# The four feature buffers of a token-mixing kernel start 32 bytes higher in each partition

## The chip, the cores and the metric

The kernel runs on one core of a Trainium2 chip. The metric is the device time of one execution in microseconds (us). Two executions of the kernel before took 2963.32 and 2964.55 us; the median is 2963.94 us.

## The reference

Three layers follow one another on x of 4 batches, 4224 tokens and 192 channels, all in float32:

```python
out = np.einsum('hk,bskhg->bshg', w, x_unf)          # 7 taps along the tokens, softmaxed
theta = x @ w_theta
zr, zi = x * np.cos(theta), x * np.sin(theta)
y = np.einsum('ts,bsd->btd', w_tok_r, zr) + np.einsum('ts,bsd->btd', w_tok_i, zi)
u = x + y; x = u + np.maximum(u @ w_ch, 0.0)
h = x.transpose(0, 2, 1) @ U @ V                     # rank 32 along the tokens
u = x + h.transpose(0, 2, 1)
out = u + np.maximum(u @ w_ch1, 0.0) @ w_ch2
```

The bulk is the token mix: two 4224 x 4224 matrices times 768 columns (4 batches of 192 channels). The weights come as float64, and the kernel turns them into float32 itself.

## The kernel before

Every large product is made of three products of halves of the numbers: a value is split into a high part (rounded to the matmul's input format, fp32r) and a low part (what is left), and high times high, high times low and low times high are added up.

**The token mix.** The 4224 source tokens are 33 blocks of 128. A unit of preparation (lines 421 to 590) takes one block and one half of the batches: the taps (L452), the product with w_theta (L515 to L519), the sine and cosine, and the rotated features z with their high and low parts (L574, L577). The features of a block go to one of four feature buffers, a pool named zp (L272), each 128 partitions by 3072 words of 4 bytes. The matrices w_tok come in by DMA, are turned from float64 into float32 by ScalarE and VectorE in four passes (L224 to L243), and are split into w (L626, L629), two buffers of 3840 words.

A step takes two blocks of source tokens and one range of 464 or 480 target tokens (WIDTHS, L34). For each of six slots of 128 columns, `products` (L671) makes twelve matmuls into one PSUM tile: z is the stationary operand, 128 x 128, loaded by an LDWEIGHTS of its own before each matmul, and w is the moving operand, 464 or 480 columns long. The twelve are four triples, in this order: z high with w high, the same z high with w low, z low with w high.

```python
for a, b in ((zh, high), (zh, low), (zl, high)):                     # L682
    mm(ps, a, b[:, i + r, :], start=n == 0, stop=n == last)          # L683
```

VectorE then adds the PSUM tile to the running sum yt (L691). The last steps of the mix are 384 wide (LATE); their weights are laid out otherwise (weight_part, L595 to L605), and between their matmuls stands the work of the layer's end: the product with w_ch (L842 to L844 and L872 to L876), the transposes (L892) and the projection by U (L912).

**The final stage** has 22 units of 384 tokens: 12 products up with w_ch1 (`up_mm`, L1165 to L1169: w stationary, the features fq moving) and 12 down with w_ch2 (`down`, L1200 to L1204: cl stationary, hid moving), five matmuls each, all 384 columns wide.

**Where the tiles lie in a partition.** Tiles are placed by pools. The pools cst, yp, wp and wraw grow from the low end, and the pools on the right side grow down from the high end: first a spacer named room (L271) that nothing reads or writes, then zp with its four buffers, then the preparation's tiles (prep), in whose place the tiles of the end of the mix (post) are put later. The tile hid lies on the left side, behind a spacer of its own (L1258).

In the following, a place is a word's number counted modulo 64 words of 4 bytes (256 bytes). In the built program the two w buffers start at byte 118496 and 133856 of a partition, both word 56 of 64. With rows of 480 words in the order of weight_part (L598), the low parts of w start at word 56 and the high parts at word 24. In the 384-wide steps, w starts at word 0 (L603); the weights of the products up start at word 8 (L605); hid starts at word 40. The four feature buffers start at bytes 180064, 192352, 204640 and 216928, all word 24, and so do all slices of 128 and 384 words in them.

Nothing sets the order of the work but the order in which it is written: the table OPENING for the first steps, the loop `mix` (L761) with a plan by slot for the middle, the tables ENTRY and TURN for the end.

Of the kernel before, what the change touches and what calls it, by code (L numbers as in the profile page):

```python
# [10 lines left out]
F32 = mybir.dt.float32  # L11
# [7 lines left out]
P = 128  # L19
# [179 lines left out]
def mix_kernel(ctx, tc, xT, wcv, wth, wtok, wch, uu, vv, w1, w2, outT):  # L199
# [3 lines left out]
    def pool(name, bufs=1, side=None, space=None, stack=None):  # L203
        kw = dict(name=name, bufs=bufs, reuse_waits="tile")
        if side:
            kw["side"] = side
        if space is not None:
            kw["space"] = space
        return (stack or ctx).enter_context(tc.tile_pool(**kw))
# [51 lines left out]
    right = ExitStack()  # L261
# [6 lines left out]
    wp = pool("wp", bufs=2, stack=left)  # L268
    wrp = pool("wraw", bufs=2, stack=raw_st)

    pool("room", side="right", stack=right).tile([P, 32], F32, name="room")  # L271
    zp = pool("zp", bufs=4, side="right", stack=right)  # L272
    pp = pool("prep", side="right", stack=prep_st)
    ps_mm = pool("ps_mm", bufs=4, space=PSUM)
# [1141 lines left out]
```

## Time and profile before

| what | value |
|---|---|
| median of two executions | 2963.94 us |
| the profiled execution | 2963.67 us |
| its span, first to last instruction | 2961.9 us |
| TensorE busy in the span | 2948.1 us, 14994 matmuls |
| weight loads busy | 2693.9 us, 14994 |
| VectorE busy | 2495.3 us |
| ScalarE busy | 1554.3 us |
| GpSimd busy | 291.8 us |
| mean granted TensorE clock | 1.000 |

PE is TensorE's matmuls and PEld its weight loads, which run beside the matmuls; DVE is VectorE, ACT is ScalarE, POOL is GpSimd. Matmuls are pipelined: the record of one goes on after the next has started, so the time that a matmul really takes from the stream is the distance from its start to the start of the next.

### The profile page before, as it was taken

Reading aid. Unit: us, or ns where it says so; the run is one execution under the profiler, and the core shown is the slowest. Engines: PE = TensorE matmul, PEld = TensorE weight load, DVE = VectorE, ACT = ScalarE, POOL = GpSimd, SP = SyncE. Lnnn points to the kernel's source line nnn. Section 1 sums busy time; section 2 is a strip of 40 time slices with the busy share of each in tenths; the row PEclk is TensorE's granted clock in tenths of the full one; section 3 lists DMA queues with packets and bytes.
Section 4 is the critical chain, followed back from the end, with each engine's and each line's share of the span. In section 5 each row is a group of like instructions: output and inputs, shape, how many; then the busy total and the mean of one; then the engine's idle time right before and its main releaser. Section 6 shows DMA issues by size and latency. Waiting matters only on the chain.

```text
span 2961.9 us, 39012 instructions
## 1 busy us (share of the span) xinstructions
PE 2948.1 (100%) x14994; PEld 2693.9 (91%) x14994; DVE 2495.3 (84%) x4133; ACT 1554.3 (52%) x2237; POOL 291.8 (10%) x254
## 2 busy tenths in 40 slices
PE   9999999999999999999999999999999999999999
PEld 8888888888888989898989898988889999999999
DVE  8799989888888888898989898989899897555555
ACT  7655545455555555554555554545456555444443
POOL 2110000010000000000000010100002002000000
PEclk9999999999999999999999999999999999999999
DMA  4443443443434434434334344343433221101110
GB/s 137 132 132 123 127 133 124 127 132 122 137 123 128 133 124 130 130 123 135 124 125 135 123 128 131 124 135 127 125 127 116 65 62 52 38 31 43 35 38 33
DMA packets 119002, 323.50 MB, mean 109 GB/s; under 512 B 6688, under 2 KB 40480, under 8 KB 118688
## 3 DMA queue, kind: packets, MB, share of 16 engines
q1 hardware_dynamic: 118416, 320.81, 33.6%
q8 instruction: 118, 1.93, 0.3%
q14 instruction: 68, 0.56, 0.1%
q10 hardware_dynamic: 400, 0.21, 0.0%
HBM read 308.01 MB, written 12.98 MB: 108 GB/s over the span
## 4 chain that ended last, share of the span: by engine, by line
PE 95%; DVE 4%; ACT 1%; issue 0%; DMA 0%; POOL 0%; DVEq 0%; POOLq 0%
PE acc L683 73%; PE ob L1201 2%; PE acc L1165 2%; PE acc L1169 2%; PE acc L1166 2%; PE oa L1202 2%; PE ob L1200 2%; PE oa L1204 2%; PE oa L1203 2%; PE acc L1167 2%; PE acc L1168 2%; PE pacc L912 1%; PE th L515 1%; PE th L516 1%; DVE yt L691 1%; PE th L518 1%
## 5 line engine op out<-in xcount | busy, mean ns | idle before, releaser
L683 PE MATMUL acc<-w,z 128*128 128x464 f32 (+2 forms) x10836 | 2287.3, 371 | 2.6 <-DVE yt L691 0.8
L683 PEld LDWEIGHTS acc<-w,z 128*128 128x128 f32 x10836 | 2018.7, 188 | 240.6 <-DVE yt L691 1.7
L691 DVE TENSOR_TENSOR yt<-acc,yt 128x464 f32<-128x464 f32 (+2 forms) x876 | 550.3, 634 | 213.3 <-PE acc L683 210.7
L626 ACT CAST w<-wraw 128x928 fp32r<-128x928 f32 (+3 forms) x291 | 303.5, 1043 | 635.1 <-DVE wraw L243 634.9
L238 DVE TENSOR_SCALAR wraw<-wraw 128x928 uint16<-128x928 uint16 (+4 forms) x305 | 368.8, 1210 | 11.8 <-ACT wraw L229 6.3
L629 DVE TENSOR_TENSOR w<-wraw,w 128x928 fp32r<-128x928 f32 (+2 forms) x282 | 365.0, 1294 | 0.0
L224 ACT ACTIVATE wraw<-wraw,consts 128x928 int32<-128x928 uint16 (+4 forms) x305 | 348.8, 1144 | 20.5 <-DMA wraw<-in_wtok 15.8
L243 DVE SCALAR_TENSOR_TENSOR wraw<-wraw 128x928 int32<-128x928 int32 (+4 forms) x305 | 342.0, 1121 | 10.1
L229 ACT ACTIVATE wraw<-wraw 128x928 f32<-128x928 f32 (+3 forms) x296 | 310.2, 1048 | 3.7 <-DMA wraw<-in_wtok 2.9
L577 POOL TENSOR_TENSOR z<-tz,z 128x384 fp32r<-128x384 f32 x121 | 125.2, 1034 | 1706.3 <-ACT z L574 1706.3
L452 DVE SCALAR_TENSOR_TENSOR xa<-xr,tap,xa 128x256 f32<-128x256 f32 x744 | 285.6, 425 | 0.0
L1177 DVE SCALAR_TENSOR_TENSOR hid<-acc,hid 128x384 fp32r<-128x384 f32 x264 | 146.9, 557 | 149.3 <-ACT hid L1174 148.3
L1174 ACT ACTIVATE hid<-acc 128x384 fp32r<-128x384 f32 x264 | 129.8, 492 | 250.2 <-PE acc L1169 233.8
L574 ACT CAST z<-tz 128x384 fp32r<-128x384 f32 x129 | 66.2, 513 | 289.4 <-DVE tz L563 289.3
L583 POOL TENSOR_TENSOR yt<-yt,xa 128x384 f32<-128x384 f32 x64 | 70.2, 1097 | 248.6 <-DVE xa L452 195.4
L1201 PE MATMUL ob<-hid,cl 128*128 128x384 f32 x264 | 89.2, 338 | 0.1
L1165 PE MATMUL acc<-fq,w 128*128 128x384 f32 x264 | 89.2, 338 | 0.0
L1169 PE MATMUL acc<-fq,w 128*128 128x384 f32 x264 | 89.0, 337 | 0.0
L1202 PE MATMUL oa<-hid,cl 128*128 128x384 f32 x264 | 88.8, 336 | 0.0
L1204 PE MATMUL oa<-hid,cl 128*128 128x384 f32 x264 | 88.8, 336 | 0.0
L1203 PE MATMUL oa<-hid,cl 128*128 128x384 f32 x264 | 88.8, 336 | 0.0
L1200 PE MATMUL ob<-hid,cl 128*128 128x384 f32 x264 | 88.7, 336 | 0.0
(239 smaller groups left out, 2655.2 us busy)
## 6 DMA issues: line engine op xcount, KB each, us to landing
wraw<-in_wtok SPq DMA_DIRECT2D x184, 928.0 KB, 4.7
wraw<-in_wtok SPq DMA_DIRECT2D x92, 960.0 KB, 4.9
wraw<-in_wtok SPq DMA_DIRECT2D x22, 768.0 KB, 4.4
xr<-in_xT SPq DMA_DIRECT2D x63, 201.0 KB, 2.6
outT<-ot SPq DMA_DIRECT2D x20, 576.0 KB, 3.0
vzw<-in_vv SPq DMA_DIRECT2D x10, 384.0 KB, 4.1
wraw<-in_w SPq DMA_DIRECT2D x3, 768.0 KB, 4.3
yt<-in_wtok SPq DMA_DIRECT2D x2, 928.0 KB, 8.8
```

What stands on the lines that cost most here:

```text
L224: nc.scalar.activation(words(raw, 0), words(raw, 1, U16), AF.Identity, scale=2.0**-13, bias=consts[:, 3:4])
L229: nc.scalar.activation(w, w, AF.Copy, scale=2.0**-112)
L238: nc.vector.tensor_scalar(out=words(raw, 1, U16), in0=words(raw, 3, U16), scalar1=0x8000, scalar2=None, op0=ALU.bitwise_and)
L243: nc.vector.scalar_tensor_tensor(out=words(raw, 1), in0=words(raw, 1), scalar=3, in1=words(raw, 0), op0=ALU.logical_shift_left, op1=ALU.bi ...
L452: nc.vector.scalar_tensor_tensor(out=xa, in0=src, scalar=w, in1=xa, op0=ALU.mult, op1=ALU.add)
L626: nc.scalar.copy(hi, src)
L629: eng.tensor_tensor(out=weight_part(g, q, 1), in0=src, in1=f(hi), op=ALU.subtract)
L683: mm(ps, a, b[:, i + r, :], start=n == 0, stop=n == last)
L691: nc.vector.tensor_tensor(out=dst, in0=ps, in1=dst, op=ALU.add)
L1165: mm(ps, w[0], q[:, b, :], start=True, stop=False)
L1169: mm(ps, w[3], q[:, 4 + b, :], start=False, stop=True)
L1201: mm(ob, c2[:, m, 2, :], h[:, 1, :], start=False, stop=last)
```

## The change

One number: the spacer on the right side is 24 words instead of 32.

```diff
-    pool("room", side="right", stack=right).tile([P, 32], F32, name="room")
+    pool("room", side="right", stack=right).tile([P, 24], F32, name="room")
     zp = pool("zp", bufs=4, side="right", stack=right)
     pp = pool("prep", side="right", stack=prep_st)
```

In the built program all tiles of zp, prep and post start 32 bytes (8 words) higher. The feature buffers start at bytes 180096, 192384, 204672 and 216960, word 32 of 64. All else stays where it was: w, wraw, yt, hid, the constants and the tiles in PSUM. No instruction is added, removed or moved on any engine or queue.

## Rows read from the trace of the kernel before

**Rows 1.** The page, part 1: busy time, share of the span, instructions.

```profile
span 2961.9 us, 39012 instructions
PE 2948.1 (100%) x14994; PEld 2693.9 (91%) x14994; DVE 2495.3 (84%) x4133; ACT 1554.3 (52%) x2237; POOL 291.8 (10%) x254
```

**Rows 2.** The waits of PE: line, whom it waited for: us, times, longest.

```profile
PE pacc L912 <- DVE u2s L902: 1.7, 5, 0.8
...
PE acc L683 <- DVE yt L691: 0.8, 1, 0.8
PE acc L683 <- POOL z L577: 0.7, 1, 0.7
```

**Rows 3.** Windows: stretch, its us, busy us and instructions by engine, granted clock, DMA.

```profile
1000.00:1100.00 100.00, 100.00 (x486) 89.12 (x485) 90.13 (x145) 52.91 (x67) 8.10 (x8) 1.00 0.40 131
...
2700.00:2800.00 100.00, 100.00 (x579) 100.00 (x578) 57.56 (x108) 44.06 (x88) 7.40 (x4) 1.00 0.13 42
```

**Rows 4.** Groups, shapes apart: count | busy us, mean ns of one | idle before.

```profile
L683 PE MATMUL acc<-w,z 128*128 128x464 f32 x6696 | 1411.5, 371 | 0.9 <-DVE yt L691 0.8
L683 PE MATMUL acc<-w,z 128*128 128x480 f32 x3348 | 731.7, 379 | 1.0 <-POOL z L577 0.7 <-ACT z L574 0.2
L683 PE MATMUL acc<-w,z 128*128 128x384 f32 x792 | 149.8, 340 | 0.7 <-DVE yt L880 0.7
L1165 PE MATMUL acc<-fq,w 128*128 128x384 f32 x264 | 89.2, 338 | 0.0
L1201 PE MATMUL ob<-hid,cl 128*128 128x384 f32 x264 | 89.2, 338 | 0.1
```

**Rows 5.** Timeline of PE, merged, mix: start us, us, line, shapes, count.

```profile
1145.82 30.28 PE L683 MATMUL acc<-w,z 128*128 128x464 f32 x144
...
1208.62 46.90 PE L683 MATMUL acc<-w,z 128*128 128x480 f32 x216
```

**Rows 6.** Groups of PE, one 464-wide triple, three windows with one record each.

```profile
L683 PE MATMUL acc<-w,z 128*128 128x464 f32 x1 | 0.4, 371 | 0.0
...
L683 PE MATMUL acc<-w,z 128*128 128x464 f32 x1 | 0.4, 367 | 0.0
...
L683 PE MATMUL acc<-w,z 128*128 128x464 f32 x1 | 0.4, 376 | 0.0
```

**Rows 7.** The same, two 480-wide triples: the distinct durations.

```profile
L683 PE MATMUL acc<-w,z 128*128 128x480 f32 x1 | 0.4, 382 | 0.0
...
L683 PE MATMUL acc<-w,z 128*128 128x480 f32 x1 | 0.4, 373 | 0.0
...
L683 PE MATMUL acc<-w,z 128*128 128x480 f32 x1 | 0.4, 379 | 0.0
...
L683 PE MATMUL acc<-w,z 128*128 128x480 f32 x1 | 0.4, 375 | 0.0
```

**Rows 8.** Timeline of PE, merged, a 384-wide step with the layer's end.

```profile
2349.37 2.25 PE L683 MATMUL acc<-w,z 128*128 128x384 f32 x12
...
2353.03 0.33 PE L872 MATMUL acc<-uz,cz 128*128 128x384 f32 x1
...
2353.90 2.28 PE L683 MATMUL acc<-w,z 128*128 128x384 f32 x12
```

**Rows 9.** DMA issues into a moved tile: count, KB each, median us to landing.

```profile
xr<-in_xT SPq DMA_DIRECT2D x63, 201.0 KB, 2.6
```

## The prediction

> **What bounds the kernel now.** I began with the busy times: PE is busy in 2948.1 of 2961.9 us [rows 1]. Next I read whom PE waited for: its longest sum is 1.7 us, and the mix line L683 shows waits of under 1 us each [rows 2]. Then the windows: the granted clock is 1.00 in the mix and in the final stage, PE is busy in all of each 100 us, and the next engine, VectorE, stands at 90.13 us in the mix and 57.56 us in the final stage [rows 3]. So the time is the sum of the distances between matmul starts, and nothing else ends last. With no instruction moved, the change can act only by making these distances longer or shorter.
>
> **What a matmul costs above its columns.** [...] An unbroken run of 144 matmuls of 464 takes 30.28 us [rows 5]; its last one lies 371 ns long in the record [rows 4], so one takes (30.28 - 0.37) / 143 = 209.2 ns: 15.9 ns above its columns. A run of 216 of 480 gives (46.90 - 0.38) / 215 = 216.4 ns, 16.4 ns above [rows 4, 5]. In both, a record is 162 ns longer than the distance to the next start (371 - 209.2, 379 - 216.4), so a single record's length, less 162 ns and less its columns, is the excess of that one matmul.
>
> Single records show that the excess depends on the operands. While one matmul streams w, the weight load of the next reads z, so each record has a pair of places: w's start and z's start. In the 464-wide triple, w high beside z high (both at word 24) lasts 371 ns, an excess of 15.7; w low (word 56) beside z low (24) lasts 367, excess 11.7; w high (24) beside the next z high (24) lasts 376, excess 20.7 [rows 6]. The mean, 16.0, agrees with the run's 15.9. In two 480-wide triples the six records last 382, 373, 379 and 382, 382, 375 ns [rows 7]: excesses of 20, 11, 17 and 20, 20, 13, mean 16.8 beside the run's 16.4. Equal starts therefore cost 18.2 ns on average at 464 and 17.5 at 480; starts half of 64 words apart cost 11.7 at 464 and 15.5 (11 and 20) at 480.
>
> Two more distances are in the rows. In the 384-wide steps w starts at word 0 and z at 24, 40 of 64 apart: (2.25 - 0.34) / 11 = 173.6 ns, 13.6 above the 160.0 of 384 columns [rows 4, 8]. In the final stage fq (24) streams beside w (8), and hid (40) beside cl (24), both 16 apart: 100 us hold 579 matmuls, 172.7 ns each, 12.7 above [rows 3].
>
> **What the change does, part by part.** It removes, adds and reorders nothing; it shifts the places of z, fq, cl, cz and the preparation's tiles by 8 words.
>
> First, the wide mix, 6696 + 3348 matmuls of L683. The pairs 24/24 become 24/32, 56 (or minus 8) of 64 apart; the pairs 56/24 become 56/32, 24 apart. No row shows either distance. For 24 I take 13.6 ns, since 16 and 40 on both sides cost 12.7 and 13.6. For 8 words from equal I take half way between equal and 13.6: 15.9 at 464, 15.6 at 480; this is a choice, an estimate from the rows named. A 464 triple then goes from 48.1 (15.7 + 11.7 + 20.7) to 15.9 + 15.9 + 13.6 = 45.4 ns, 2.7 less; 2232 triples give 6.0 us. A 480 triple goes from 50.5 (half of 101 for the six) to 15.6 + 15.6 + 13.6 = 44.8, 5.7 less; 1116 triples give 6.4 us.
>
> Second, the 792 matmuls of the 384-wide steps go from 40 to 32 apart. The rows for 32 are 11.7 and 15.5, mean 13.6: no change. The 1320 products up go from 16 to 24 apart, again 13 or so on either side: no change. The 1320 products down go from 16 to 8 apart. Equal starts at 384 columns are to be seen where uz and cz are read (both at 24): the five from L872 to L876 take 2353.90 - 2353.03 = 0.87 us, 174 ns each, 14.0 above [rows 8]. Half way from 12.7 to 14.0 is 0.65 ns more, times 1320 is 0.9 us lost.
>
> Third, what isn't on the path. VectorE's and ScalarE's work on moved tiles hides below PE: of each 100 us VectorE has 9.9 idle in the mix [rows 3]. If its work on them grew beyond that, PE would begin to wait in L683 for the additions of L691. The 63 loads of xr land 2.6 us after issue [rows 9] and are issued five slots ahead, each slot 12 matmuls of over 200 ns, so over 12 us: hidden. I cost all of this at nothing.
>
> The sum is -6.0 - 6.4 + 0.9 = -11.5 us. The profiled execution took 2963.67 us, 0.27 below the median 2963.94, so both give 2952 us.
>
> **Bounds.** From below: the whole wide mix at the cheapest 464 record, 11.7 ns, is 6696 x 4.2 + 3348 x 4.7 = 44 us less, 2920 us. From above: all of it at the dearest frequent 480 record, 20 ns, is 6696 x 4.1 + 3348 x 3.6 = 40 us more, 3003 us.
>
> **The rivals.** (a) *The starts don't matter.* Then the differences between records come from something else that repeats with the triple, such as the order high, low, high, and the time stays 2964 us. For it: w high beside z at equal places costs 15.7 once and 20.7 once, and a w low row costs 11 in one 480 triple and 20 in the other although its place modulo 64 is the same [rows 6, 7]; the pair of places alone doesn't explain the records. Equal starts at 384 cost only 14.0 [rows 8]. Against it: the lower 464 record is the one whose starts differ. [...]
>
> (b) *The new pairs are the dear ones.* [...] It decides from a mean excess above 16.1 ns in the wide mix on. For it: all six 480 records range between 11 and 20 with so little that differs between them, and nothing in the rows covers 24 or 56 apart. Against it: the rows at 16 and 40 apart lie at 12.7 and 13.6.
>
> (c) *Beyond every row.* Slower by over 2%, 59 us, needs 5.9 ns more on each of the 10044 wide matmuls, a mean of 22 ns; only single records come near. Faster by over 2% needs a mean of about 10.2 ns, below the cheapest record of 11.
>
> **How the numbers follow.** I give the forecast, a small gain between some 5 and 44 us, 0.40; rival (a), within 5 us, 0.25; rival (b), slower by 5 to 59 us, 0.22; (c) beyond 2% slower 0.09, beyond 2% faster 0.04. The point is that of the forecast, 2952 us. The range takes the two bounds, 2920 to 3003 us, which leaves a little under 2 in 10 outside, since the likely excesses lie within the rows. The likeliest case has a range of its own, 2920 to 2959 us. A measurement can tell about 2% from no change; within that lie the forecast, (a) and (b), 0.87 together.
>
> **What would show it.** In the changed profile the run of 144 matmuls of 464 should take about 30.16 us (0.9 ns less each) and the run of 216 of 480 about 46.5 us (1.9 less). By (a) they stay 30.28 and 46.90; by (b) they go to about 30.87 and 47.7. The records of a triple should draw together: w high to about 371 and w low to 369 ns at 464. The final stage should keep about 579 matmuls in 100 us. PE should still wait for nobody; a sum of waits of over 5 us in L683 would mean that VectorE's work on moved tiles grew, and that the argument looked at the wrong engine. The forecast is wrong if the runs lengthen, or if they shorten to below 29.7 us (464), which needs less than 11.7 ns a matmul.

## The result and the profile after

The changed kernel takes 2998.25 us (median of 2997.71 and 2998.79), the kernel before 2963.94 us: a ratio of 1.0114, 95% interval 1.0098 to 1.0131. It is slower by 34 us, less than 2%. The forecast of a small gain was wrong in sign.

The page of the changed kernel, part 1 (columns as in [rows 1]):

```profile
span 2997.0 us, 39012 instructions
PE 2983.2 (100%) x14994; PEld 2700.6 (90%) x14994; DVE 2497.7 (83%) x4133; ACT 1553.8 (52%) x2237; POOL 291.3 (10%) x254
```

PE is busy 35.1 us longer with the same 14994 matmuls; the weight loads beside them are busy 6.7 us longer, VectorE, ScalarE and GpSimd as long as before, within 2.4 us. No wait of PE grew by more than 0.4 us (the first of these rows stood at 1.6 us before):

```profile
PE tr L892 <- DVE u2s L902: 2.0, 4, 1.0
...
PE acc L683 <- POOL z L577: 0.8, 1, 0.8
...
PE acc L683 <- DVE yt L691: 0.5, 1, 0.5
```

The groups of matmuls of the changed kernel (count | busy us, mean ns of one | idle before), which answer [rows 4], say where the 35 us are:

```profile
L683 PE MATMUL acc<-w,z 128*128 128x464 f32 x6696 | 1432.9, 374 | 0.5 <-DVE yt L691 0.5
L683 PE MATMUL acc<-w,z 128*128 128x480 f32 x3348 | 738.0, 381 | 1.1 <-POOL z L577 0.8 <-ACT z L574 0.3
L683 PE MATMUL acc<-w,z 128*128 128x384 f32 x792 | 150.4, 340 | 0.7 <-DVE yt L880 0.7
```

Beside [rows 4], the 464-wide matmuls of the mix take 21.4 us more (1432.9 - 1411.5), the 480-wide 6.3 us (738.0 - 731.7), the 384-wide 0.6 us. The rest is the final stage: 100 us hold 570 matmuls where they held 579 [rows 3]:

```profile
1000.00:1100.00 100.00, 100.00 (x482) 88.28 (x481) 88.70 (x142) 53.67 (x70) 10.14 (x10) 1.00 0.39 123
2700.00:2800.00 100.00, 100.00 (x570) 100.00 (x569) 59.15 (x111) 46.88 (x92) 9.28 (x5) 1.00 0.10 32
```

That is 175.4 instead of 172.7 ns each, 2.7 ns on some 2640 products, 7.1 us, an estimate from one stretch. The sum is 35.4 us; PE's busy time rose by 35.1. The granted clock is 1.00 in both stretches.

The runs of the mix without a break, as in [rows 5]:

```profile
1158.64 30.74 PE L683 MATMUL acc<-w,z 128*128 128x464 f32 x144
...
1222.36 47.31 PE L683 MATMUL acc<-w,z 128*128 128x480 f32 x216
```

What the columns alone take, the matmuls alone of the experiments show: from its first start to the next run's, a cheapest run of 24 took 4.16 us at 384 columns (1352.85 to 1357.01 in the grid below), 4.96 at 464 and 5.12 at 480 (123.81 to 128.77 and 169.89 to 175.01 under the shorter loads), so 173.3, 206.7 and 213.3 ns a matmul. That is 40.0 ns for 96 columns, 0.417 ns a column, and the 464 lie on the same line. Columns of 160.0, 193.3 and 200.0 ns are worked out from this, an estimate that takes the cheapest excess, 13.3 ns, to be equal at the three widths.

With these, (30.74 - 0.37) / 143 = 212.4 ns, an excess of 19.0 above the columns where it was 15.9; (47.31 - 0.38) / 215 = 218.3, an excess of 18.3 where it was 16.4. This is rival (b), nearly at its price for 464 (30.87 us for the run of 144).

The three records of one 464-wide triple of the changed kernel, taken as those of [rows 6] were:

```profile
L683 PE MATMUL acc<-w,z 128*128 128x464 f32 x1 | 0.4, 371 | 0.0
...
L683 PE MATMUL acc<-w,z 128*128 128x464 f32 x1 | 0.4, 374 | 0.0
...
L683 PE MATMUL acc<-w,z 128*128 128x464 f32 x1 | 0.4, 375 | 0.0
```

They drew together, as the prediction had it, but at the dear end: the cheap record of w low, 367 ns before, is gone.

### The profile page after: what moved, and what is told of

It reads as the page before. It is cut to its first block, busy times and chain, and to the rows that moved or that the text cites. A ratio compares the mean times of both kernels' runs of the same rounds, so it can differ in the third digit from the quotient of the medians.

```text
span 2997.0 us, 39012 instructions
## 1 busy us (share of the span) xinstructions
PE 2983.2 (100%) x14994; PEld 2700.6 (90%) x14994; DVE 2497.7 (83%) x4133; ACT 1553.8 (52%) x2237; POOL 291.3 (10%) x254
## 4 chain that ended last, share of the span: by engine, by line
PE 95%; DVE 3%; DMA 1%; ACT 1%; issue 0%; SPq 0%; POOL 0%; DVEq 0%; ACTq 0%
PE acc L683 73%; PE acc L1166 2%; PE ob L1200 2%; PE acc L1165 2%; PE ob L1201 2%; PE acc L1167 2%; PE acc L1168 2%; PE oa L1204 2%; PE oa L1203 2%; PE acc L1169 2%; PE oa L1202 2%; PE pacc L912 1%; PE th L515 1%; PE th L516 1%; PE th L518 1%; PE tr L892 1%
## 5 line engine op out<-in xcount | busy, mean ns | idle before, releaser
L683 PE MATMUL acc<-w,z 128*128 128x464 f32 (+2 forms) x10836 | 2315.7, 374 | 2.3 <-POOL z L577 0.8
L691 DVE TENSOR_TENSOR yt<-acc,yt 128x464 f32<-128x464 f32 (+2 forms) x876 | 551.1, 635 | 237.9 <-PE acc L683 235.2
L224 ACT ACTIVATE wraw<-wraw,consts 128x928 int32<-128x928 uint16 (+4 forms) x305 | 349.0, 1144 | 22.0 <-DMA wraw<-in_wtok 17.7
L1166 PE MATMUL acc<-fq,w 128*128 128x384 f32 x264 | 89.8, 340 | 0.0
L1165 PE MATMUL acc<-fq,w 128*128 128x384 f32 x264 | 89.5, 339 | 0.0
L1204 PE MATMUL oa<-hid,cl 128*128 128x384 f32 x264 | 89.2, 338 | 0.0
L1167 PE MATMUL acc<-fq,w 128*128 128x384 f32 x264 | 89.1, 338 | 0.0
L1168 PE MATMUL acc<-fq,w 128*128 128x384 f32 x264 | 89.1, 337 | 0.0
```

What stands on the lines that cost most here:

```text
L224: nc.scalar.activation(words(raw, 0), words(raw, 1, U16), AF.Identity, scale=2.0**-13, bias=consts[:, 3:4])
L691: nc.vector.tensor_tensor(out=dst, in0=ps, in1=dst, op=ALU.add)
L1165: mm(ps, w[0], q[:, b, :], start=True, stop=False)
L1166: mm(ps, w[0], q[:, 2 + b, :], start=False, stop=False)
```

## The experiments

Three theories stood at the start. D: the two read streams of TensorE, the weight load's and the moving operand's, interfere, and the distance of their starts decides how much. Z: the place of z alone decides. O: other engines' reads and writes slow TensorE.

### Matmuls alone, at every pair of places

The kernel has two resident tiles and nothing but weight loads and matmuls from them:

```python
    for n in (464, 480, 384):
        for zp in PLACES:                      # 0, 8, ... 56
            for wp in range(0, 128, 8):
                ...                            # 24 pairs of starts: z at zp, w at wp
                a = run(f"n{n}z{zp}w{wp}e", pairs, n)
...                                            # and for 464 and 480, z at 0 to 120:
                pairs += [(zh, hi), (zh, lo), (zl, hi)]     # 24 times, so 72 matmuls
```

> A kernel that does nothing of the reference but matmuls: one weight load and one matmul after another from two resident tiles, no other engine at work meanwhile. Runs of 24 at every pair of places (z at 0 to 56 of 64, w at 0 to 120 of 128) for 464, 480 and 384 columns, and the triples of the mix (w high at 24, low at 56) for every place of z. Theory D (the two read streams of TensorE meet each other, and the distance of their starts decides): the excess above the columns is the same along lines of equal distance, differs between them by several ns, and the triples give about 15.9 ns at z 24 and 19.2 at z 32 with 464 columns. Theory Z (the place of z alone decides): the excess differs by rows of z and not by w. Theory O (TensorE is slowed by what other engines and DMAs read and write): every run has the same excess, some 3 to 12 ns, whatever the places.

The timeline of PE, merged (start us, us, line, tile, shapes, count); the tile's name says the columns and the places, so n464z24w56e is 464 columns, z at 24, w at 56 (a constant run), and t464z24e is the triple of the mix with z at 24:

```profile
286.30 5.18 PE L46 MATMUL n464z24w24e<-w,z 128*128 128x464 f32 x24
...
306.53 5.22 PE L46 MATMUL n464z24w56e<-w,z 128*128 128x464 f32 x24
...
367.31 5.13 PE L46 MATMUL n464z32w24e<-w,z 128*128 128x464 f32 x24
...
387.41 5.27 PE L46 MATMUL n464z32w56e<-w,z 128*128 128x464 f32 x24
...
1352.85 4.33 PE L46 MATMUL n384z0w16e<-w,z 128*128 128x384 f32 x24
1357.01 4.40 PE L46 MATMUL n384z0w24e<-w,z 128*128 128x384 f32 x24
...
1365.47 4.40 PE L46 MATMUL n384z0w40e<-w,z 128*128 128x384 f32 x24
...
1912.55 15.36 PE L46 MATMUL t464z16e<-w,z 128*128 128x464 f32 x72
1927.74 15.20 PE L46 MATMUL t464z24e<-w,z 128*128 128x464 f32 x72
1942.78 15.44 PE L46 MATMUL t464z32e<-w,z 128*128 128x464 f32 x72
...
2064.21 15.44 PE L46 MATMUL t464z96e<-w,z 128*128 128x464 f32 x72
...
2156.14 15.99 PE L46 MATMUL t480z16e<-w,z 128*128 128x480 f32 x72
2171.97 15.76 PE L46 MATMUL t480z24e<-w,z 128*128 128x480 f32 x72
2187.57 15.89 PE L46 MATMUL t480z32e<-w,z 128*128 128x480 f32 x72
```

With the record's length taken off as before, the triple costs an excess of (15.20 - 0.37) / 71 - 193.3 = 15.5 ns with z at 24 and 18.9 with z at 32 for 464 columns, and 16.6 and 18.5 for 480. The kernels' runs gave 15.9 and 19.0, 16.4 and 18.3. No other engine worked meanwhile:

```profile
200.00:300.00 100.00, 100.00 (x477) 89.04 (x476) 0.00 (x0) 0.00 (x0) 0.00 (x0) 1.00 0.00 0
```

So O falls. The loss in the mix is TensorE's own, and the grid gives it to within 0.4 ns a matmul. The place counts modulo 64: the triple with z at 96 takes the same 15.44 us as with z at 32. Over the whole grid of constant runs the means, from start to start after the first eight, repeat along lines of equal distance; for 464 columns, z at 0 and w at 64, 72, ... 120, they are 15.6, 17.7, 16.5, 19.9, 17.7, 19.1, 20.0 and 13.3 ns above the columns, and each further row of z has the same numbers shifted by one place. (The first runs of a row are off by up to 1.2 ns; why isn't shown.)

What the grid took away from the prediction is its price list. In constant runs w high beside z before, 24/24, costs (5.18 - 0.37) / 23 - 193.3 = 15.8 ns, and w low beside z, 56/24, costs 17.5: the reverse of the single records, where the equal start was dear and the half distance cheap. At 480 columns the order is that of the records: 16.4 and 13.3 after the first eight. The new 24/32 is among the cheapest at 464, 13.6, and 56/32 among the dearest, 19.7. If pairs had prices, the new triple would cost (13.6 + 13.6 + 19.7) / 3 = 15.6; it costs 18.9.

For 384 columns the same reckoning gives (4.33 - 0.34) / 23 - 160.0 = 13.5 ns at 16 words apart, but 16.5 at 24 and at 40. The products up go from 16 to 24 apart, so the grid has them dearer.

### Both streams up by 8 words

```diff
+    pool("lead", stack=left).tile([P, 8], F32, name="lead")
     wp = pool("wp", bufs=2, stack=left)
```

on top of the change: w, wraw and hid move with z, fq and cl.

> The changed kernel with a spacer of 8 words ahead of w too, so that w, wraw and hid also start 8 words higher: all distances between z and w, fq and w, hid and cl are those of before, only the places differ. Theory D: 2964 us, runs of 144 matmuls of 464 at 30.28 us. Theory Z: 2998 us, 30.74 us. Theory O: between them or 2998.

2962.67 us, beside 2964.47 for the kernel before on the same chip; the runs of the mix as before. (One execution of each; thirteen of the kernel before, taken later on another chip, lie between 2962.12 and 2965.67 us.)

```profile
1113.64 30.28 PE L684 MATMUL acc<-w,z 128*128 128x464 f32 x144
...
1207.80 46.90 PE L684 MATMUL acc<-w,z 128*128 128x480 f32 x216
```

z lies at word 32 as in the changed kernel, and the whole loss is gone. Z falls: word 32 is no worse than word 24; what was lost was the distance to the other stream. The two rows are, to the hundredth, those of [rows 5].

### Only w up, and z further up

The same spacer on the kernel before, so that z stays at 24:

```diff
+    pool("lead", stack=left).tile([P, 8], F32, name="lead")
     wp = pool("wp", bufs=2, stack=left)
```

> The kernel before (z at word 24) with w, wraw and hid 8 words higher: w high at 32, low at 0, hid at 48. Distances of w from z are 8 and 40 where before has 0 and 32 and the changed kernel 56 and 24. Theory D: neither 2964 nor 2998 by need, but what the triple of distances 8 and 40 gives in the grid. Theory Z: 2964 us, since z stays at 24. Theory O: 2964.

2992.71 us: z has not moved, and 28 us are lost. The distances of this triple are those of the grid's triple with z at 16, whose excess is 17.8 ns at 464 and 20.0 at 480 (here and below from start to start after the first eight). From 15.6 and 16.6 at z 24 this gives 6696 x 2.2 = 14.7 and 3348 x 3.4 = 11.4 us. The groups of this kernel rose by 14.1 (1425.6 - 1411.5) and 11.1 us (742.8 - 731.7); the rest is about what the final stage lost, which holds 573 matmuls in 100 us:

```profile
L684 PE MATMUL acc<-w,z 128*128 128x464 f32 x6696 | 1425.6, 373 | 0.2 <-DVE yt L692 0.2
L684 PE MATMUL acc<-w,z 128*128 128x480 f32 x3348 | 742.8, 382 | 1.1 <-POOL z L578 0.8 <-ACT z L575 0.3
```

And the spacer of 16 words, which puts z at 40:

```diff
-    pool("room", side="right", stack=right).tile([P, 24], F32, name="room")
+    pool("room", side="right", stack=right).tile([P, 16], F32, name="room")
```

> The changed kernel with a spacer of 16 words: z at word 40 of 64, w as before, distances 48 and 16. If the excess grows with how far z is moved up from 24, this is slower than 2998 us; if z at 32 is a single bad place, near 2964; the grid's triple at z 40 tells which, by theory D.

2969.23 us, with runs of 30.27 and 46.91 us: the mix costs what it did at 24, as the grid's 15.6 and 16.7 for z at 40 say, and of the 5 us more some 3 are the final stage's (575 matmuls in 100 us, 1.2 ns more on 2640) and 1.1 the 384-wide steps' (150.9 us busy, before 149.8). So there is no slope upwards from 24; z at 32 lies between two good places.

### The final stage held at its distances

```diff
-            return t[:, 2 * WSTEP * q + 16 : 2 * WSTEP * q + 16 + 2 * COLS]
+            return t[:, 2 * WSTEP * q + 24 : 2 * WSTEP * q + 24 + 2 * COLS]
...
-            fo.tile([P, 112], F32, name="room", tag="room")
+            fo.tile([P, 120], F32, name="room", tag="room")
```

on top of the change: the weights of the products up, and hid, move by 8 words too.

> The changed kernel (z at 32), with the weights of the products up 8 words higher and hid 8 words higher: in the final stage the distances of before, 16, come back; the mix stays as changed. Theory D: what the final stage lost, 570 instead of 579 matmuls in 100 us over its 2640 products up and down, some 6 to 7 us, is won back: 2991 us; the wide runs stay at 30.74 and 47.31 us. Theory Z: 2998 us.

2991.07 us, 7.2 less than the changed kernel. In the final stage 579 matmuls fit in 100 us again, and the run of 144 stays at 30.74 us:

```profile
2700.00:2800.00 100.00, 100.00 (x579) 100.00 (x578) 60.54 (x114) 46.34 (x92) 9.28 (x5) 1.00 0.10 34
```

The loss of 34 us is thus split by a run: 7 us in the final stage, 27 in the mix.

### Two places forecast from the grid

Without the spacer z starts at word 56, with one of 56 words at word 0; in both kernels the weights of the products up and hid are moved so that the final stage keeps its distance of 16. For z at 56:

```diff
-    pool("room", side="right", stack=right).tile([P, 24], F32, name="room")
...
-            return t[:, 2 * WSTEP * q + 16 : 2 * WSTEP * q + 16 + 2 * COLS]
+            return t[:, 2 * WSTEP * q + 48 : 2 * WSTEP * q + 48 + 2 * COLS]
...
-            fo.tile([P, 112], F32, name="room", tag="room")
+            fo.tile([P, 144], F32, name="room", tag="room")
```

For z at 0 the spacer is 56 words, the offset in the second edit 56 and the third 88.

> No spacer: z at word 56, with the final stage held at its distances of 16. The grid's triples give 15.5 ns at both widths for z 56, where z 24 gave 15.6 and 16.6. Theory D: 6696 x -0.1 and 3348 x -1.1 ns from 2964 us: 2960 us, runs of 144 and 216 of 30.27 and 46.7 us. Theory Z: not to be said.

> A spacer of 56 words: z at word 0, the final stage again held at 16. The grid's triples give 20.0 ns at 464 and 18.9 at 480, the dearest place for 464. Theory D: 6696 x 4.4 + 3348 x 2.3 ns = 37 us above 2964: 3001 us, runs of 30.9 and 47.4 us.

They took 2959.61 and 2998.63 us, 0.4 and 2.4 us off what the grid had foretold. z at 56, then z at 0:

```profile
1144.00 30.27 PE L682 MATMUL acc<-w,z 128*128 128x464 f32 x144
...
1206.79 46.68 PE L682 MATMUL acc<-w,z 128*128 128x480 f32 x216
```

```profile
1130.78 30.91 PE L683 MATMUL acc<-w,z 128*128 128x464 f32 x144
...
1226.78 47.37 PE L683 MATMUL acc<-w,z 128*128 128x480 f32 x216
```

The kernel with z at 56 was timed again in three rounds:

> z at word 56 with the final stage at its distances of 16, timed against the kernel before. Theory D: the 4 to 5 us of the first look stay, a ratio of 0.9984. If the first look was chance: 1.000.

2959.29 us beside 2963.70, a ratio of 0.9985, interval 0.9975 to 0.9994. It beats both kernels, by 0.15% and 1.3%; of its gain of 4.4 us on the kernel before, 3.0 us are in the 480-wide steps (728.7 us busy instead of 731.7), as forecast.

### Shorter loads, and other layouts

> Matmuls alone again, nothing of the reference. First, constant runs with weight loads of 128, 64 and 32 columns at eight distances, 464 and 480 columns moving. Theory D (the load's read stream and the moving stream meet): with 64 columns to load the spread over the distances, 13.3 to 20 ns with 128, shrinks to about half, with 32 to about a quarter, and the lowest value falls too. Theory Z' (only the start addresses cost, some fixed time at the beginning of a load): the spread stays near 7 ns whatever the load's length. Second, triples in which the low part lies at 0 to 56 words from the high part and every other block's row at 0 or 32: if distances alone decide, some layout comes near the lowest constant run, 13.3 ns, in both widths, where the kernel's layout gives 15.6 and 16.6.

The edit: constant runs whose stationary operand has 64 or 32 columns (m64, m32 in the names), and triples with other distances of the low part.

```profile
58.38 5.27 PE L46 MATMUL n464m128w48e<-w,z 128*128 128x464 f32 x24
63.49 5.13 PE L46 MATMUL n464m128w56e<-w,z 128*128 128x464 f32 x24
...
93.64 5.13 PE L46 MATMUL n464m64w40e<-w,z 128*64 128x464 f32 x24
...
108.65 5.28 PE L46 MATMUL n464m32w0e<-w,z 128*32 128x464 f32 x24
...
123.81 5.12 PE L46 MATMUL n464m32w24e<-w,z 128*32 128x464 f32 x24
128.77 5.21 PE L46 MATMUL n464m32w32e<-w,z 128*32 128x464 f32 x24
...
169.89 5.28 PE L46 MATMUL n480m128w32e<-w,z 128*128 128x480 f32 x24
175.01 5.39 PE L46 MATMUL n480m128w40e<-w,z 128*128 128x480 f32 x24
...
2017.49 10.93 PE L46 MATMUL t480r0h40d24e<-w,z 128*128 128x480 f32 x48
```

A miss for D as I had pictured it. With 32 columns to load, the dearest and the cheapest of eight runs of 24 still lie 0.16 us apart (5.28 and 5.12), with 128 columns 0.14 (5.27 and 5.13); the lowest excess stays at 13.3 ns. So the cost isn't a number of meetings in proportion to what the load reads. Z' had the spread right. But at 464 the cheapest distance moves with the load's length (56 words with 128 columns, 40 with 64, 24 among others with 32), so the starts alone don't set the cost either. No run leaves the load out, so how much of the 13.3 ns is its doing isn't shown. Of the 128 triples tried in each width, the best for the kernel's mixture of widths (15.4 ns at both) would save 1 us over z at 56; no layout came near 13.3 at both widths, a second miss. The dearest triple lies above every constant run: (10.93 - 0.39) / 47 - 200.0 = 24.3 ns, with w high at 40 and w low 24 words further.

### The order of the triple

> Matmuls alone, nothing of the reference: the triple in three orders (high-high, high-low, low-high as in the kernel; high-high, low-high, high-low; high-low, high-high, low-high), w low 32 words from w high, z low at 0 to 56 words from z high, eight places of w. If each pair of places had a price of its own, the order would change nothing: the mean of a triple would be the same in all three orders. If a matmul's delay depends on what went before it, the orders differ by some ns at the same places. A layout with a mean near 13.3 ns in both widths would be worth 10044 x 2.3 ns = 23 us to the kernel; the layouts so far stop at 15.5.

```profile
219.86 10.35 PE L46 MATMUL o464p0h16z24e<-w,z 128*128 128x464 f32 x48
...
1019.79 10.19 PE L46 MATMUL o464p1h32z16e<-w,z 128*128 128x464 f32 x48
...
1514.73 10.09 PE L46 MATMUL o464p2h16z24e<-w,z 128*128 128x464 f32 x48
...
1666.62 10.39 PE L46 MATMUL o464p2h32z16e<-w,z 128*128 128x464 f32 x48
...
2482.70 10.41 PE L46 MATMUL o480p0h48z8e<-w,z 128*128 128x480 f32 x48
...
3819.88 10.61 PE L46 MATMUL o480p2h48z8e<-w,z 128*128 128x480 f32 x48
```

The name gives the columns, the order (p0 as in the kernel, p1 with its last two swapped, p2 high-low first), w high's distance from z high, and z low's. The same three matmuls at the same places cost (10.35 - 10.09) / 47 = 5.5 ns a matmul less in another order, and at 480 columns (10.61 - 10.41) / 47 = 4.3 ns more.

This alone doesn't refute a price for w's start with that of the z loaded beside it, which is the pair that the prediction meant: with z low elsewhere than z high, another order also loads another z beside each w. The grid's triples refute it, where all of z lies at one place (15.6 by prices, 18.9 measured). So does a comparison inside this run. Repeated, p1 and p2 are one and the same cycle, begun at another member. In most layouts they cost the same; but with w high at 32 and z low at 16 they lie (10.39 - 10.19) / 47 = 4.3 ns a matmul apart, with the same places in the same sequence. A pair of places has no price of its own: what a matmul costs depends on what came before it, and even on how the run began.

Some layouts reach 13.4 ns at one width, none at both; the best, w high at 16 and z low at 24 in order p2, gives 13.4 at 464 and 17.0 at 480, some 9 us below z at 56 over the wide mix, by these prices. It wasn't tried in the kernel, where z low would need 24 words more in each feature buffer and a stride of the buffers that keeps their places.

## Why the prediction was wrong

**What bounds the kernel** was right. PE's waits stayed within 0.4 us, the clock stayed at 1.00, and the time moved by what the distances between matmul starts moved.

**The cost above the columns** was read rightly as a mean: 15.9 and 16.4 ns, which matmuls alone reproduce as 15.5 and 16.6. No row ahead of the prediction shows what it took off for the columns; the matmuls alone showed it afterwards, 0.417 ns a column, which gives the same 193.3, 200.0 and 160.0 ns.

**The price of a pair** is the step that failed: "Equal starts therefore cost 18.2 ns on average at 464 and 17.5 at 480; starts half of 64 words apart cost 11.7 at 464 and 15.5 (11 and 20) at 480." Within a triple, one record's delay and the next one's belong together, and only the sum over a repeating triple is a cost. At 464 constant runs of the same pairs have the reverse order (15.8 and 17.5), their prices put the new triple at 15.6 where it costs 18.9, and the same cycle of places costs 4.3 ns more or less by how it began. The warning was in the rows and was named under rival (a): the same pair 24/24 at 15.7 and 20.7 in one triple. It was used against the size of the effect and not against the price list.

**The interpolation** built on it: 15.9 for a start 8 words off and 13.6 for 24 words. Over the places of 8 words the excess isn't smooth at all: in constant runs of 464 columns neighbouring distances jump from 13.3 to 20.0 ns. There was nothing to interpolate; 24 apart, taken as the cheapest, is one of the dearest (19.9 at 464, 20.0 at 480). The forecast of -6.0 and -6.4 us became +21.4 and +6.3.

One of its two supports was also misread. The 13.6 for 40 words apart came from a single 384-wide step of 2.25 us; the other step in [rows 8], of 2.28 us, gives (2.28 - 0.34) / 11 - 160.0 = 16.4, and the grid's constant run at 40 apart 16.5.

**The 384-wide steps**, forecast at no change, took 0.6 us more. **The products up and down**: forecast at 0 and 0.9 us lost, together they lost 7. It is the same interpolation: "13 or so on either side" for the products up, 24 apart, where the grid has 16.5. What the products down lost, 8 apart, the constant runs don't show (13.3 ns at 8 as at 16); that part stays open.

**What isn't on the path** stayed off it, as forecast: VectorE's busy time rose by 2.4 us, and the waits for the additions of L691 went from 0.8 to 0.5 us.

**The rivals.** (a) fell, since both_up_8 and the grid show that the starts matter: in the grid z's place alone moves a constant run of 464 columns between 13.3 and 20.0 ns with no other engine at work. (b) held, in its direction and nearly in its price: the mix at 19.0 and 18.3 ns against the 20 that its runs of 30.87 and 47.7 us suppose. That 2998 us came so near 3003, the time with the whole wide mix at 20 ns, is in part luck, since that prices the mix alone, which lost 28 of those 40 us (21.4 + 6.3), and the final stage added 7. Why the new pairs are dear is not shown: the distance of the two starts moves the excess between 13.3 and 20.0 ns, but loads of 32 columns leave the spread of a run at 0.16 us where 128 have 0.14. What makes the excess is left open. (c) did not come up; the range of 2920 to 3003 held the time, though its upper bound, 20 ns for every wide matmul, was no limit (24.3 ns in one triple above).

## What to carry to other kernels

In this kernel, which the matmuls bound (PE busy in 2948.1 of 2961.9 us) and where loads and matmuls follow one another without a gap, the place of each operand within 64 words was a tuning knob of about 1% (2959.29 us with z at 56, 2998.63 with z at 0), and it acted by the distance of the stationary from the moving operand: z's side moved alone by 8 words cost 34 us, w's side alone 28. A tile that is moved for any reason changed it for all that streams beside it, as the final stage's 7 us show. It couldn't be read from single records or interpolated; a kernel that does nothing but the real sequence of matmuls, at each of eight places, foretold two kernels to within 3 us and accounts for the mix of two more. Moving both operands by the same 8 words cost nothing (2962.67 us beside 2964.47), so a spacer on the other side repaired what a moved tile had spoilt.

## What the runs showed of the hardware that I had not expected

Matmuls alone, fp32r with a weight load each at a granted clock of 1.00, cost 13.3 to 20.0 ns above their columns in constant runs, by the distance of the two starts modulo 64 words. At 0.417 ns a column the lowest and the highest are the time of 32 and 48 columns, at 464 and at 480 columns alike. With 32 columns to load the lowest is 13.3 ns again. What a matmul costs isn't set by its own pair alone: within a run of one pair the records differ (370 to 375 ns at 464 columns with z and w at 24), the same three matmuls in another order differ by up to 5.5 ns each, and one cycle of places can settle at two costs, 4.3 ns apart (runs of 10.39 and 10.19 us).
